# Another order of all units in a sorted-block attention and gated MLP kernel, with other PSUM banks and copying engines

## The chip, the core and the metric

The kernel runs on one core of one Trainium2 chip. A core has a matrix engine (TensorE, "PE"), a vector engine (VectorE, "DVE"), a scalar engine (ScalarE, "ACT"), GpSimd ("POOL") and a queue engine (SyncE, "SP"); each runs its own instruction stream in order, and the streams wait for each other by semaphores. TensorE writes its results to PSUM, eight banks, from which VectorE or ScalarE must copy them out before a bank can be used again. The metric is the device time of one execution in microseconds, less is better.

## The reference

Two layers, one after the other. First, attention within sorted blocks (batch 4, 8 heads, 768 tokens, head size 64, 8 blocks of 96 tokens): a small 8x8 matrix P per head is made from `sort_net`, and it mixes the blocks of K and V; each block of queries then attends to its mixed block.

```python
for _ in range(5):
    P = exp(P - max(P)); P = P / P.sum(-1); P = P / P.sum(-2)
k_sorted = einsum('bhij,bhjcd->bhicd', P, k_b); v_sorted = einsum(..., P, v_b)
attn = softmax(scale * q_b @ k_sorted^T)   # per block
x = (attn @ v_sorted)                      # 4 x 768 x 512
h = relu(x @ w_in); u, v = h[..., :512], h[..., 512:]
v_n = (v - mean(v)) / sqrt(var(v) + 1e-6)
v_s = w_spatial @ v_n + b_spatial          # over the tokens
out = (u * v_s) @ w_out
```

Inputs and outputs are float32; matmuls run on bfloat16.

## The kernel before, in words

The kernel is written as small *units*, each a Python function `u_XX`. The string `ORDER` at line 18 lists them, with arguments; `run` (line 805) calls them one by one, and nothing reorders the instructions afterwards, so on every engine an instruction stands where its unit stands in the string. A unit with matmuls names its PSUM place first (0 to 3 are pairs of banks, 10 to 17 single banks, of which 10 and 11 are pair 0, 12 and 13 pair 1, and so on), then the engine that copies the result out (A for ScalarE, D for VectorE), then the batch and the part. For example `UP:2:A:0:0:1` makes one block of U in pair 2, and ScalarE takes it out.

The units, in the order in which one batch needs them:

- `S0`, `SK`: load `sort_net`, then five rounds of normalising it on VectorE with an exp on ScalarE (line 248). `DM` (line 236) runs dummy matmuls on a tile `warm` meanwhile. `PR` (line 266) spreads P, `P0` (line 280, VectorE, batch 0) and `PD` (line 292, GpSimd, the other batches, from `prep_sb`, which `PC` copies) build the mixing matrices `pd`.
- `L`, `LH`: loads. All `L` loads are issued by GpSimd and cast to bfloat16 on the way (line 177 for q, k and v; 182 and 185 for the two halves of `w_in`, `wv` and `wu`; 191 for the two halves of `w_spatial`; 194 for `w_out`). `BI` (line 206) loads the bias `b_bc`.
- q, turned: batches 0 and 1 by TensorE (`QT`, line 325); batches 2 and 3 by a copy `QP` into `qp` (line 374, through the helper at line 122 or 124) and one DMA transpose `QX` on the SP queue (line 381).
- `KT` (line 394): K mixed and turned, 24 matmuls, into `kt_all`.
- V, mixed: batch 0 by `VT` and `VB` (lines 394 and 412); the others by `VM` (line 421) into `vm`, and `VC`, eight small DMAs on the SP queue (line 434), into `vb`.
- `SC` (line 453): scores of one head pair and half, then the exp on ScalarE (line 458) into one of five `ex_all` tiles. `AT` (line 499): attention times V, divided by its sum on VectorE (lines 506 and 507), into `x_sb`.
- x, turned: batch 0 by TensorE (`XT`, line 529), the others by DMA transposes `XD` on the SP queue (line 517).
- `VP`, `VH` (line 566): the V half of the first layer for one tile of tokens, then relu. `ST` (lines 586 and 587), `LN` (592, 593) and `LA` (598): the normalisation. `UP` (line 612): the U half. `WT`, `WW` (lines 535 and 542): the spatial weights, turned.
- `SP` (line 624): the spatial layer, then the bias on VectorE (line 630) into `z`. `GT` (line 641): times U, on VectorE or GpSimd. `OP` (line 650): the output layer, `OE` copies it out, `OS` (line 665) stores it, on the SP queue or, with a last `A`, from ScalarE's.
- The last batch's end is cut finer: `SH`, `GH`, `OH`, `OI`, `OJ` (lines 680, 693, 700, 707 to 714, 718).

The batches overlap: while batch b goes through the MLP, batch b + 1 is in attention, and the string interleaves them by hand-set numbers. The helpers `copy` (lines 120 to 124) and `relu` (126 to 130) hold most copies out of PSUM, so their rows carry those lines.

```python
    def run(order):
        for item in order.split():
            name, *args = item.split(":")
            units[name](*args)
```

Of the kernel before, what the change touches and what calls it, by code (L numbers as in the profile page):

```python
# [15 lines left out]

ORDER = """
S0 CO LH:A:0 TB L:q:0:4:8 SK:0 DM:10:3:384 DM:10:4:512 DM:10:13:512 BH ID IV:0 L:v:0:0:8 MC MA SK:1 DM:10:4:256 SK:2
QC:A:0 SK:3 SK:4 QC:A:1 QT:10:A:0:2 IV:2 QT:11:A:0:3 DM:12:4:512 QT:12:A:0:0 DM:13:6:512 PR:10 MB P0:0:2 P0:2:4  # L20
VT:2:A:0:0 VT:3:D:0:1 P0:4:6 QT:11:A:0:1 P0:6:8 VB:13:A:0:0 VB:12:D:0:1 L:k:0:0:8 PC:A VT:2:A:0:2 KT:3:D:0:1
KT:1:A:0:2 KT:0:A:0:3 VT:2:D:0:3 SC:3:0:1:1 KT:1:D:0:0 SC:0:0:2:0 VB:14:D:0:2 SC:3:0:3:0 L:k:1:0:8 AT:1:0:1:1
SC:0:0:0:0 L:v:1:0:8 PD:1:0:4 VB:15:D:0:3 SC:3:0:1:0 AT:1:0:2:0 SC:0:0:2:1 AT:2:0:3:0 SC:3:0:0:1 PD:1:4:8 AT:1:0:0:0
KT:0:A:1:0 XT:14:D:0:0:2 AT:3:0:0:1 SC:1:0:3:1 KT:0:A:1:3 AT:2:0:2:1 VM:1:A:1:0 AT:3:0:3:1 VM:0:A:1:1 VM:2:D:1:3
L:q:1:0:8 VM:1:A:1:2 XT:16:A:0:1:2 L:wv AT:0:0:1:0 XT:17:A:0:1:0 KT:2:D:1:1 KT:1:A:1:2 QT:16:D:1:1 QT:10:D:1:3
QT:11:A:1:2 QT:17:D:1:0 XT:14:D:0:0:0 SC:1:1:1:0 L:wsa SC:0:1:2:1 SC:3:1:2:0 VP:15:D:0:4 ST:0:4 VP:14:D:0:3 L:wu
SC:1:1:0:0 SC:0:1:1:1 VP:15:D:0:1 L:wsb ST:0:3 WT:16:A:1 WT:17:D:0 VP:14:A:0:0 ST:0:1 VH:15:A:0:2 ST:0:0 WT:16:A:2
VC:1:0:4 L:q:2:0:8 VH:17:A:0:5 VC:1:4:8 PD:2:0:4 ST:0:2 ST:0:5 AT:1:1:0:0 LN:0:0:6 AT:0:1:1:0 UP:2:A:0:0:0
UP:3:A:0:1:0 BI LA:0:3 LA:0:4 AT:1:1:2:0 SC:2:1:0:1 UP:0:A:0:1:1 LA:0:1 AT:3:1:2:1 L:v:2:0:8 WT:14:A:3 L:k:2:0:8
LA:0:5 LA:0:2 WW:1:D:4 LA:0:0 SC:0:1:3:1 SC:3:1:3:0 UP:2:A:0:0:1 PD:2:4:8 AT:0:1:3:1 QP:A:2:0 SP:1:0:3 QP:A:2:3  # L30
AT:3:1:3:0 QP:A:2:2 AT:2:1:0:1 QP:A:2:1 SP:0:0:0 AT:1:1:1:1 SP:3:0:2 VM:2:A:2:2 XD:1:0 VM:0:A:2:1 GT:D:0:0 SP:1:0:1
VM:3:D:2:0 GT:P:0:1 VM:2:A:2:3 VH:10:A:1:0 ST:1:0 KT:1:A:2:0 KT:2:D:2:1 KT:3:A:2:3 QX:2:0:4 KT:0:D:2:2 XD:1:1
UP:1:A:1:1:0 VH:16:D:1:1 SC:2:2:2:0 SC:0:2:0:0 VC:2:0:4:0:4 ST:1:1 GT:P:0:2 SC:1:2:3:0 VH:17:D:1:3 L:wo UP:2:A:1:1:1
AT:0:2:2:0 VH:16:A:1:4 AT:1:2:0:0 GT:P:0:3 VH:17:D:1:5 SC:2:2:1:0 L:q:3:0:8 SC:0:2:0:1 SC:1:2:1:1 VH:16:A:1:2 ST:1:3
UP:2:A:1:0:0 ST:1:5 AT:0:2:3:0 ST:1:4 ST:1:2 UP:1:A:1:0:1 LN:1:0:6 OP:3:0:2:2 LA:1:5 LA:1:1 SC:2:2:3:1 L:v:3:0:8
SC:0:2:2:1 PD:3:4:8 LA:1:0 OP:1:0:4:2 PD:3:0:4 LA:1:3 LA:1:2 OE:A:0:2 LA:1:4 L:k:3:0:8 QP:D:3:0 VC:2:4:8:0:4 OE:A:0:4
AT:2:2:3:1 SP:0:1:3 QP:A:3:3 AT:3:2:1:0 AT:1:2:2:1 QP:A:3:1 SP:2:1:1 AT:0:2:1:1 QP:A:3:2 VM:3:A:3:1 OP:1:0:0:2
OE:D:0:0 OS:0:0:0:1:A OS:0:0:1:2:A VM:2:A:3:3 AT:3:2:0:1 SP:0:1:2 VM:1:A:3:0 GT:P:1:1 XD:2:0 VM:3:D:3:2 SP:2:1:0
VH:16:D:2:2 QX:3:0:4 KT:0:A:3:0 KT:1:D:3:2 KT:2:D:3:3 KT:3:A:3:1 XD:2:1 VH:10:D:2:0 SC:1:3:0:1 ST:2:2 SC:3:3:0:0
SC:2:3:3:1 VC:3:4:8:0:4 OS:0:4:0:1 OS:0:4:1:2 VH:11:D:2:4 VH:10:A:2:5 AT:1:3:0:1 GT:P:1:3 VH:16:D:2:3 ST:2:3 ST:2:5  # L40
GT:P:1:2 SC:2:3:1:1 SC:0:3:2:1 SC:1:3:1:0 VH:17:A:2:1 GT:D:1:0 UP:2:A:2:1:0 AT:0:3:2:1 UP:1:A:2:1:1 ST:2:1 AT:3:3:1:1
ST:2:4 AT:2:3:3:1 UP:0:A:2:0:1 ST:2:0 UP:1:A:2:0:0 VC:3:0:4:0:4 AT:3:3:0:0 LN:2:0:6 LA:2:2 OP:0:1:0:2 OE:A:1:0 LA:2:4
AT:2:3:1:0 OP:1:1:4:2 LA:2:5 SC:3:3:2:0 LA:2:0 LA:2:3 LA:2:1 SC:0:3:3:0 OP:2:1:2:2 AT:3:3:3:0 SP:0:2:1 GT:D:2:1
OE:A:1:4 XD:3:1 AT:1:3:2:0 SP:3:2:0 SP:0:2:2 CK XD:3:0 GT:P:2:0 OE:A:1:2 SP:2:2:3 VH:1:D:3:5:3 GT:D:2:3 VH:10:D:3:4
UP:3:A:3:1:1 CF:11 VH:12:A:3:2 VH:13:A:3:1 OS:1:2:0:1 OS:1:2:1:2 LF VH:16:A:3:0 GT:D:2:2 OS:1:0:0:1:A OS:1:0:1:2:A
UP:2:A:3:1:0 ST:3:1 ST:3:3 UP:0:A:3:0:0 ST:3:4 ST:3:5 OP:1:2:0:2 ST:3:2 ST:3:0 OP:3:2:4:2 LN:3:0:6 LA:3:3 OE:D:2:0
LA:3:4 OP:2:2:2:2 LA:3:0 LA:3:1 OE:A:2:2 LA:3:5 UP:0:A:3:0:1 OE:A:2:4 LA:3:2 OS:0:2:0:1 OS:0:2:1:2 SH:12:3:2:0
SH:13:3:3:0 GH:P:3:3:0 SH:16:3:0:0 GH:D:3:2:0 SH:17:3:1:0 GH:P:3:0:0 SH:16:3:1:1 SH:12:3:2:1 OS:2:4 GH:P:3:1:0
SH:13:3:3:1 OS:2:0 GH:D:3:1:1 SH:17:3:0:1 OS:1:4 GH:D:3:3:1 OS:2:2 GH:P:3:0:1 GH:P:3:2:1 IF OH:16:3:2:0:512:0:4
OI:A:3:2:0:512 OH:12:3:3:0:512:0:4 OH:13:3:0:0:512:0:4 OI:D:3:0:0:512 OI:A:3:3:0:512 OH:17:3:1:0:512:0:4  # L50
OJ:3:2:0:512:S OJ:3:3:0:512:A OI:A:3:1:0:512 OJ:3:0:0:512:S OH:16:3:4:256:512:0:4 OI:D:3:4:256:512 OH:12:3:5:0:256:0:4
OI:D:3:5:0:256 OJ:3:1:0:512:S OJ:3:4:256:512:A OH:13:3:5:256:512:0:4 OJ:3:5:0:256:S OI:D:3:5:256:512
OH:17:3:4:0:128:0:4 OH:10:3:4:128:256:0:4 OI:B:3:4:0:256 OJ:3:5:256:512:S OJ:3:4:0:256:A
"""

# [791 lines left out]
```

## Time and profile before

| what | value |
|---|---|
| time, median of 3 runs (lowest, highest) | 149.85 us (149.81, 150.05) |
| the profiled execution's own time | 150.1 us |
| its span | 148.2 us |
| VectorE, ScalarE, GpSimd busy in the span | 114.6, 85.7, 39.1 us |
| granted TensorE clock | 1.0 of full |
| DMA moved | 25.94 MB, 175 GB/s on average |

How to read it: the page gives busy times of the engines, the span cut into 40 slices, and the chain of work that ended last, followed back from the last instruction. Further views list the instructions of one engine in order of time, the groups by line, the waits by what ended them, and each DMA's time from issue to landing. Times of rows are microseconds from the start of the span. A row that ends in square brackets tells how long the engine had been idle ahead of it and whom it waited for. TensorE's weight loads are counted apart (PEld).

### The profile page before, as it was taken

To read this page: it belongs to the slowest core of one execution; us is meant where nothing else is said; L and a number is where in the kernel's file an instruction comes from. 1 tells how busy PE (TensorE), PEld (TensorE's weight loads), DVE (VectorE), ACT (ScalarE), POOL (GpSimd) and SP (SyncE) were. 2 spreads that over 40 slices of the span, in tenths; PEclk is the share of its full clock that TensorE was granted. 3 is DMA by queue.
4 is the path that set the end of the run, shared out by engine and by line. 5 is a ranking of instruction groups with operands and counts; after the bars stand their busy time and mean duration, and the time that the engine had idled before them with its cause. 6 is when DMAs were issued, how large, how long until landed. Compare 5 with 4: busy or idle time off the path is not lost.

```text
span 148.2 us, 4112 instructions
## 1 busy us (share of the span) xinstructions
PE 142.2 (96%) x1689; PEld 101.1 (68%) x1691; DVE 114.6 (77%) x262; ACT 85.7 (58%) x126; POOL 39.1 (26%) x44
## 2 busy tenths in 40 slices
PE   6997999999999999999999999999999999999991
PEld 2355877866776667777877678768866876864760
DVE  3876899979987887867869779899558989846741
ACT  5347998997689546659693328756640046160040
POOL 6700599500000005992001640000002100004630
PEclk9999999999999999999999999999999999999999
DMA  3999999999999999799999999503602607007766
GB/s 93 263 203 204 204 208 201 209 218 242 234 248 216 209 215 237 110 172 221 205 201 178 206 243 286 118 0 73 38 0 56 194 3 283 2 2 264 296 224 221
DMA packets 37014, 25.94 MB, mean 175 GB/s; under 512 B 16704, under 2 KB 34112, under 8 KB 36992
## 3 DMA queue, kind: packets, MB, share of 16 engines
q0 software_dynamic: 14432, 12.19, 51.6%
...
q8 instruction: 14, 0.23, 0.6%
...
## 4 chain that ended last, share of the span: by engine, by line
PE 90%; DVE 6%; ACT 1%; issue 1%; DVEq 0%
PE ps L624 16%; PE ps L566 15%; PE ps L612 14%; PE ps L650 11%; PE ps L236 6%; PE ps L680 5%; PE ps L499 4%; PE ps L394 4%; PE ps L453 4%; PE ps L700 4%; PE ps L421 3%; DVE x_sb L507 2%; PE ps L325 2%; DVE vb L124 1%; PE ps L535 1%; PE ps L529 1%
## 5 line engine op out<-in xcount | busy, mean ns | idle before, releaser
L641 POOL TENSOR_TENSOR gt<-z,u_sb 128x768 bf16<-128x768 f32 x7 | 11.4, 1644 | 68.8 <-DVE z L630 55.5
L458 ACT ACTIVATE ex_all<-ps 96x768 bf16<-96x768 f32 x32 | 23.7, 807 | 5.0 <-PE ps L453 4.0
L624 PE MATMUL ps<-wspT,v_sb 128*128 128x384 bf16 x144 | 25.0, 326 | 0.0
L566 PE MATMUL ps<-w_in_sb,xT 128*128 128x256 bf16 (+1 forms) x175 | 23.7, 282 | 0.1
L612 PE MATMUL ps<-xT,w_in_sb 128*128 128x384 bf16 x128 | 23.0, 326 | 0.0
L128 ACT ACTIVATE u_sb<-ps 128x768 bf16<-128x768 f32 x16 | 13.0, 811 | 17.3 <-PE ps L612 17.2
L507 DVE TENSOR_TENSOR x_sb<-ps,rec_all 96x512 bf16<-96x512 f32 x32 | 22.0, 686 | 1.1
L624 PEld LDWEIGHTS <-v_sb 128*128 128x128 bf16 x144 | 13.5, 98 | 8.4
L566 PEld LDWEIGHTS <-xT 128*128 128x128 bf16 x176 | 16.3, 98 | 4.0
L650 PE MATMUL ps<-w_out_sb,gt 128*128 128x256 bf16 x144 | 16.9, 273 | 0.0
L612 PEld LDWEIGHTS <-w_in_sb 128*128 128x128 bf16 x128 | 12.0, 98 | 7.0
L586 DVE BATCH_NORM_STATS2 stats<-v_sb 128x6 f32<-128x512 bf16 x24 | 16.2, 675 | 0.6 <-ACT v_sb L128 0.5
L122 ACT COPY o_sb<-ps 128x1024 f32<-128x1024 f32 (+2 forms) x11 | 8.9, 830 | 12.6 <-PE ps L700 9.3
L630 DVE TENSOR_TENSOR z<-ps,b_bc 128x768 f32<-128x768 f32 x12 | 11.5, 954 | 5.9 <-PE ps L624 5.1
L650 PEld LDWEIGHTS <-gt 128*128 128x128 bf16 x144 | 13.8, 98 | 2.0
L499 PEld LDWEIGHTS <-ex_all 96*128 96x128 bf16 x256 | 11.1, 97 | 2.6
L499 PE MATMUL ps<-vb,ex_all 96*128 96x65 bf16 x256 | 12.3, 193 | 0.1
L122 ACT CAST vm<-ps 128x768 bf16<-128x768 f32 x9 | 6.8, 807 | 9.7 <-PE ps L421 6.6
L236 PE MATMUL ps<-warm 128*128 128x512 bf16 (+2 forms) x33 | 9.6, 451 | 1.3 <-DVE warm L210 1.3
L693 POOL TENSOR_TENSOR gt<-z,u_sb 128x512 bf16<-128x512 f32 (+1 forms) x5 | 5.2, 1047 | 21.5 <-DVE z L686 21.5
L506 DVE RECIPROCAL rec_all<-ps 96x8 f32<-96x8 f32 x32 | 6.3, 196 | 5.5 <-PE ps L499 5.3
L130 DVE TENSOR_SCALAR v_sb<-ps 128x512 bf16<-128x512 f32 (+1 forms) x12 | 8.7, 727 | 1.6 <-PE ps L566 1.5
...
## 6 DMA issues: line engine op xcount, KB each, us to landing
...
vb<-vm SPq DMA_DIRECT2D x24, 99.0 KB, 4.7
...
```

What stands on the lines that cost most here:

```text
L122: nc.scalar.copy(out=out, in_=in_)
L128: nc.scalar.activation(out=out, in_=in_, func=AF.Relu)
L236: nc.tensor.matmul(t[:, 0, 0:int(w)], lhsT=warm[:, 0:128], rhs=warm[:, 0:int(w)], start=True, stop=True)
L458: nc.scalar.activation(out=e_tile(b, hp, ih).rearrange("p h (x g) -> p h x g", g=G), in_=t[0:BLK, :, 0:HW].rearrange("p h (g x) -> p h x g ...
L499: nc.tensor.matmul(t[:, hh, ii * VW:ii * VW + D + 1], lhsT=e[:, c:c + 128], rhs=vb[b % 2][:, ih * NI + ii, 2 * hp + hh, 0:D + 1], start=Tr ...
L507: nc.vector.tensor_mul(out=x_sb[:, hp].rearrange("p i (h d) -> p h i d", h=2), in0=tv[:, :, :, 0:D], in1=_raw_ap(rec, 0, [rec.ap[0], [NI, ...
L566: nc.tensor.matmul(t[:, x, c:c + DH // parts], lhsT=st["xT", b][:, n // 3, kc, (n % 3) * 128:(n % 3 + 1) * 128], rhs=w_in_sb[:, kc, DH + c ...
L586: nc.vector.bn_stats(out=stats, in_=st["v_sb", b, n])
L612: nc.tensor.matmul(t[:, x, 0:HW], lhsT=w_in_sb[:, kc, mc * 128:(mc + 1) * 128], rhs=st["xT", b][:, ih, kc, :], start=(kc == 0), stop=(kc = ...
L624: nc.tensor.matmul(t[:, x, 0:HW], lhsT=st["v_sb", b, n][:, mc * 128:(mc + 1) * 128], rhs=wspT[:, 3 * x:3 * x + 3, n, :], start=(n == 0), s ...
L630: nc.vector.tensor_add(out=z.rearrange("p (x c) -> p x c", x=2), in0=t[:, :, 0:HW], in1=b_bc.rearrange("p (x c) -> p x c", x=2),)
L650: nc.tensor.matmul(t[:, x, c:c + w], lhsT=st["gt", b, mc][:, (n0 + x) * 128:(n0 + x + 1) * 128], rhs=w_out_sb[:, mc, c:c + w], start=(mc = ...
```

## The change

Only the string `ORDER` differs. The same work is listed in another sequence, with other banks and other copying engines: against before, ScalarE has two `KT` more, two of the `UP` less, and VectorE one `VB`, one `QT`, one `XT` and the `PC` copy more, and four single-tile and the one double relu of the V half less. The dummies `DM` are regrouped. `WW`, which turned two parts of the spatial weights into one pair, is two `WT`. Stores of the first batches that stood on the SP queue stand in ScalarE's stream, later. `L:wv` and `L:wu` stand next to each other. The core of the diff, its first and fourth line:

```diff
-S0 CO LH:A:0 TB L:q:0:4:8 SK:0 DM:10:3:384 DM:10:4:512 DM:10:13:512 BH ID IV:0 L:v:0:0:8 MC MA SK:1 DM:10:4:256 SK:2
+S0 CO IV:0 DM:10:3:384 DM:10:3:512 IV:2 LH:A:0 TB SK:0 L:q:0:4:8 BH ID MA DM:10:12:512 SK:1 DM:10:1:128 SK:2 QC:A:0
...
-L:q:1:0:8 VM:1:A:1:2 XT:16:A:0:1:2 L:wv AT:0:0:1:0 XT:17:A:0:1:0 KT:2:D:1:1 KT:1:A:1:2 QT:16:D:1:1 QT:10:D:1:3
+XT:15:D:0:1:0 VM:3:A:1:0 VM:1:A:1:2 XT:14:D:0:0:2 L:wv L:wu VM:0:D:1:1 XT:15:D:0:0:0 KT:3:A:1:1 QT:14:D:1:3
```

Three places, as the instructions stand on the engines. First VectorE behind the last round on P (`p_t`), up to the copies of the first K and V tiles (`-` before, `+` now, neither: in both):

```order
 L261 STREAM_TRANSPOSE p_t<-p_75 32x64
+L124 COPY qT<-ps 128x768
 L224 CAST mask_89<-m_88 128x16
-L280 TENSOR_TENSOR pd<-mask_89,ps 128x256 x2
+L280 TENSOR_TENSOR pd<-mask_89,ps 128x256 x4
+L124 CAST prep_sb<-ps 128x256
 L124 CAST vt_all<-ps 128x768
-L280 TENSOR_TENSOR pd<-mask_89,ps 128x256 x2
 L124 COPY vb_97<-ps 96x8x2x64
-L124 CAST kt_all<-ps 128x768
+L124 CAST kt_all<-ps 128x768 x2
+L124 COPY vb_97<-ps 96x8x2x64
```

A qT copy now stands ahead of the mask; the four `P0` stand together with the `prep_sb` copy behind them and ahead of the first `vt_all`.

Second, GpSimd's loads in the middle of the start, from the mixing matrices of batch 1 to the load of q for batch 2:

```order
-L292 TENSOR_TENSOR pd<-mask_89,prep_sb 128x512 x2
+L292 TENSOR_TENSOR pd<-mask_89,prep_sb 128x512 x3
 L177 DMA q_in<-in_q_dram 128x8x384
 L182 DMA w_in_sb<-in_moe_w_in_dram 128x4x512
-L191 DMA ws_in<-in_moe_w_spatial_dram 128x3x768
 L185 DMA w_in_sb<-in_moe_w_in_dram 128x4x512
-L191 DMA ws_in<-in_moe_w_spatial_dram 128x3x768
+L191 DMA ws_in<-in_moe_w_spatial_dram 128x3x768 x2
+L206 DMA b_bc<-in_moe_b_spatial_dram 128x768
 L177 DMA q_in<-in_q_dram 128x8x384
```

The two halves of `w_in` are still two instructions, now one behind the other; both halves of `w_spatial` and the bias follow; a third half of `pd` is made ahead of them.

Third, ScalarE around the copies of q for batch 3 (`qp`) and its V (`vm`), before:

```order
L592 ACTIVATE rstd<-mv,eps 128x6
L593 ACTIVATE rstd<-rstd 128x6
L458 ACTIVATE ex_all<-ps 96x768 x2
L122 COPY o_sb<-ps 128x1024 x2
L122 COPY qp<-q_in 128x2x6x64 x3
L122 CAST vm<-ps 128x2x6x64
L665 DMA out_dram<-o_sb 128x512 x2
L122 CAST vm<-ps 128x2x6x64 x2
```

and now:

```order
L122 COPY o_sb<-ps 128x1024
L458 ACTIVATE ex_all<-ps 96x768
L122 COPY qp<-q_in 128x2x6x64
L128 ACTIVATE u_sb<-ps 128x2x384
L122 CAST vm<-ps 128x2x6x64
L122 COPY qp<-q_in 128x2x6x64
L122 CAST vm<-ps 128x2x6x64
L122 COPY qp<-q_in 128x2x6x64
L122 CAST vm<-ps 128x2x6x64
```

The three `qp` copies of ScalarE (VectorE makes the fourth in both) stood together ahead of V; now they alternate with the `vm` copies, and the last stands behind the second of these. The two stores are gone from here.

More of the change, by code (lines that the diff above doesn't have):

```diff
@@ L18 @@
 ORDER = """
-S0 CO LH:A:0 TB L:q:0:4:8 SK:0 DM:10:3:384 DM:10:4:512 DM:10:13:512 BH ID IV:0 L:v:0:0:8 MC MA SK:1 DM:10:4:256 SK:2
[L20 to L23, printed above, removed]
@@ L24 @@
-KT:0:A:1:0 XT:14:D:0:0:2 AT:3:0:0:1 SC:1:0:3:1 KT:0:A:1:3 AT:2:0:2:1 VM:1:A:1:0 AT:3:0:3:1 VM:0:A:1:1 VM:2:D:1:3
-L:q:1:0:8 VM:1:A:1:2 XT:16:A:0:1:2 L:wv AT:0:0:1:0 XT:17:A:0:1:0 KT:2:D:1:1 KT:1:A:1:2 QT:16:D:1:1 QT:10:D:1:3
-QT:11:A:1:2 QT:17:D:1:0 XT:14:D:0:0:0 SC:1:1:1:0 L:wsa SC:0:1:2:1 SC:3:1:2:0 VP:15:D:0:4 ST:0:4 VP:14:D:0:3 L:wu
-SC:1:1:0:0 SC:0:1:1:1 VP:15:D:0:1 L:wsb ST:0:3 WT:16:A:1 WT:17:D:0 VP:14:A:0:0 ST:0:1 VH:15:A:0:2 ST:0:0 WT:16:A:2
-VC:1:0:4 L:q:2:0:8 VH:17:A:0:5 VC:1:4:8 PD:2:0:4 ST:0:2 ST:0:5 AT:1:1:0:0 LN:0:0:6 AT:0:1:1:0 UP:2:A:0:0:0
@@ L29 @@
[L29 to L53, printed above, removed]
+S0 CO IV:0 DM:10:3:384 DM:10:3:512 IV:2 LH:A:0 TB SK:0 L:q:0:4:8 BH ID MA DM:10:12:512 SK:1 DM:10:1:128 SK:2 QC:A:0
@@ new lines @@
+SK:3 SK:4 MC QT:10:A:0:2 QT:11:A:0:3 DM:12:13:512 L:v:0:0:8 QT:12:D:0:0 PR:10 MB DM:11:2:256 P0:0:2 P0:2:4 P0:4:6
+QC:A:1 VT:2:A:0:0 P0:6:8 QT:11:A:0:1 PC:D VT:3:D:0:1 VB:13:D:0:0 L:k:0:0:8 VT:2:A:0:3 KT:0:D:0:1 KT:3:A:0:3 KT:1:D:0:2
+KT:2:A:0:0 SC:0:0:1:1 VB:16:D:0:1 SC:1:0:3:0 VT:2:D:0:2 SC:0:0:3:1 VB:17:D:0:3 L:k:1:0:8 SC:1:0:0:0 L:v:1:0:8 PD:1:0:4
+AT:2:0:1:1 SC:0:0:0:1 PD:1:4:8 VB:16:D:0:2 SC:1:0:2:0 PD:2:0:4 AT:2:0:3:0 KT:0:A:1:3 AT:3:0:0:0 SC:1:0:2:1 AT:2:0:3:1
+KT:0:A:1:0 AT:3:0:0:1 SC:1:0:1:0 AT:2:0:2:1 L:q:1:0:8 KT:0:A:1:2 AT:3:0:2:0 VM:1:A:1:3 XT:14:A:0:1:2 AT:0:0:1:0
@@ new lines @@
+XT:15:D:0:1:0 VM:3:A:1:0 VM:1:A:1:2 XT:14:D:0:0:2 L:wv L:wu VM:0:D:1:1 XT:15:D:0:0:0 KT:3:A:1:1 QT:14:D:1:3
+QT:12:A:1:1 L:wsa QT:13:D:1:2 L:wsb QT:10:D:1:0 SC:3:1:3:0 SC:2:1:1:0 BI L:q:2:0:8 SC:1:1:2:0 SC:0:1:3:1 VP:16:D:0:1
+VP:17:A:0:5 ST:0:1 VP:14:D:0:2 VP:15:A:0:0 VH:16:A:0:4 VH:17:A:0:3 UP:1:A:0:0:1 ST:0:5 WT:16:A:2 WT:17:A:1 ST:0:0
+ST:0:2 ST:0:4 L:v:2:0:8 VC:1:0:4 ST:0:3 AT:0:1:1:0 AT:2:1:3:0 UP:1:D:0:1:0 LN:0:0:6 LA:0:4 SC:0:1:0:1 LA:0:0 LA:0:3
+SC:3:1:2:1 UP:2:A:0:0:0 WT:10:D:4 WT:11:A:3 AT:1:1:2:0 VC:1:4:8 WT:16:D:5 LA:0:1 WT:17:A:0 SC:2:1:0:0 SC:0:1:1:1
@@ new lines @@
+LA:0:2 UP:1:A:0:1:1 LA:0:5 QP:A:2:0 AT:3:1:2:1 QP:A:2:2 L:k:2:0:8 SP:2:0:0 QP:A:2:1 AT:0:1:0:0 AT:3:1:3:1 SP:1:0:1
+PD:2:4:8 AT:2:1:0:1 XD:1:0 AT:0:1:1:1 SP:3:0:3 GT:P:0:3 VM:1:D:2:1 QP:A:2:3 VM:2:A:2:3 SP:0:0:2 L:wo VM:3:A:2:0
+VM:2:A:2:2 VH:12:A:1:0 VH:13:D:1:1 KT:3:A:2:2 QX:2:0:4 KT:0:A:2:3 L:v:3:0:8 KT:2:D:2:1 KT:1:A:2:0 ST:1:1 VH:16:D:1:2
+GT:D:0:1 PD:3:4:8 SC:0:2:1:0 XD:1:1 PD:3:0:4 SC:2:2:2:0 VC:2:0:4:0:4 SC:1:2:3:0 VH:17:D:1:4 VH:0:A:1:5:3 ST:1:2 ST:1:5
+UP:2:A:1:1:0 SC:3:2:3:1 ST:1:4 SC:1:2:0:0 VC:2:4:8:0:4 GT:D:0:2 GT:P:0:0 UP:0:A:1:0:1 ST:1:0 ST:1:3 UP:2:A:1:1:1
@@ new lines @@
+LN:1:0:6 AT:3:2:2:0 OP:1:0:0:2 AT:0:2:1:0 LA:1:0 AT:2:2:3:0 LA:1:5 OP:3:0:2:2 OE:A:0:0 SC:1:2:1:1 SC:0:2:2:1 LA:1:1
+OP:2:0:4:2 LA:1:3 L:q:3:0:8 OE:A:0:4 OE:D:0:2 AT:1:2:0:0 L:k:3:0:8 SC:0:2:0:1 LA:1:4 QP:A:3:1 UP:3:A:1:0:0 VM:2:A:3:2
+LA:1:2 QP:D:3:2 AT:1:2:1:1 SP:0:1:2 QP:A:3:0 VM:3:A:3:1 AT:2:2:3:1 SP:1:1:1 XD:2:0 AT:0:2:0:1 AT:3:2:2:1 QP:A:3:3
+SP:2:1:0 QX:3:0:4 GT:P:1:1 VM:1:A:3:0 VM:0:D:3:3 VH:16:A:2:2 XD:2:1 KT:2:A:3:3 KT:1:A:3:2 KT:0:D:3:0 KT:3:D:3:1
+SP:2:1:3 VH:10:A:2:1 ST:2:2 VC:3:4:8:0:4 SC:1:3:3:1 SC:3:3:0:1 SC:2:3:2:1 VC:3:0:4:0:4 VH:11:A:2:4 VH:10:A:2:5
@@ new lines @@
+GT:D:1:2 AT:1:3:3:1 GT:P:1:3 ST:2:1 UP:3:A:2:1:0 GT:D:1:0 VH:14:D:2:3 SC:1:3:1:0 SC:0:3:1:1 ST:2:3 SC:3:3:0:0
+VH:15:A:2:0 OP:1:1:0:2 ST:2:4 ST:2:5 AT:0:3:2:1 OE:A:1:0 ST:2:0 AT:3:3:1:1 UP:2:A:2:0:0 LN:2:0:6 LA:2:0 LA:2:4
+OP:1:1:2:2 OE:A:1:2 LA:2:2 AT:0:3:0:1 LA:2:5 UP:2:D:2:1:1 LA:2:1 LA:2:3 SC:3:3:3:0 SC:1:3:2:0 UP:0:A:2:0:1 AT:2:3:3:0
+OS:0:2:0:1:A OS:0:2:1:2:A AT:3:3:0:0 OS:0:4:0:1:A OS:0:4:1:2:A SP:1:2:3 AT:0:3:1:0 SP:2:2:2 AT:3:3:2:0 OS:1:2:0:1:A
+OS:1:2:1:2:A GT:D:2:2 XD:3:1 SP:1:2:1 XD:3:0 UP:0:A:3:0:1 GT:D:2:3 CK SP:2:2:0 OP:3:1:4:2 VH:10:A:3:3 CF:11
@@ new lines @@
+VH:1:A:3:0:1 VH:11:D:3:5 ST:3:3 GT:P:2:0 ST:3:1 OE:A:1:4 ST:3:0 VH:2:A:3:4:2 GT:P:2:1 OP:1:2:4:2 UP:0:A:3:1:1 ST:3:2
+UP:3:A:3:1:0 LF ST:3:4 ST:3:5 LN:3:0:6 LA:3:5 OE:A:2:4 LA:3:0 LA:3:4 OS:1:0:0:1:A OS:1:0:1:2:A OP:2:2:2:2 LA:3:2
+LA:3:1 OE:A:2:2 LA:3:3 OP:0:2:0:2 OE:A:2:0 OS:0:0:0:1 OS:0:0:1:2 UP:3:A:3:0:0 SH:14:3:2:0 SH:15:3:3:0 GH:P:3:3:0
+SH:14:3:0:0 GH:D:3:2:0 SH:15:3:1:0 GH:P:3:0:0 SH:14:3:1:1 SH:16:3:2:1 OS:2:4 GH:P:3:1:0 SH:15:3:3:1 OS:2:0 GH:D:3:1:1
+SH:14:3:0:1 OS:1:4 GH:D:3:3:1 OS:2:2 GH:P:3:0:1 GH:P:3:2:1 IF OH:17:3:2:0:512:0:4 OI:A:3:2:0:512 OH:16:3:3:0:512:0:4
@@ L54 @@
+OH:15:3:0:0:512:0:4 OI:D:3:0:0:512 OI:A:3:3:0:512 OH:14:3:1:0:512:0:4 OJ:3:2:0:512:S OJ:3:3:0:512:A OI:A:3:1:0:512
+OJ:3:0:0:512:S OH:17:3:4:256:512:0:4 OI:D:3:4:256:512 OH:16:3:5:0:256:0:4 OI:D:3:5:0:256 OJ:3:1:0:512:S
+OJ:3:4:256:512:A OH:15:3:5:256:512:0:4 OJ:3:5:0:256:S OI:D:3:5:256:512 OH:14:3:4:0:128:0:4 OH:10:3:4:128:256:0:4
+OI:B:3:4:0:256 OJ:3:5:256:512:S OJ:3:4:0:256:A
 """
```

## The prediction

> **What bounds the kernel now.** I read the page first, then the chain of work that ended last, because it says on which engine a saving would count.
>
> ```profile
> span 148.2 us, 4112 instructions
> PE 142.2 (96%) x1689; PEld 101.1 (68%) x1691; DVE 114.6 (77%) x262; ACT 85.7 (58%) x126; POOL 39.1 (26%) x44
> PE   6997999999999999999999999999999999999991
> ```
>
> TensorE is busy for 96% of the span, and its slices show the only thin places: the first four of forty and the last. The chain, in order of time (start, length, what), says where that begins:
>
> ```profile
> 1.28 7.15 PE ps L236 x24
> 8.43 0.79 PE ps L325 x24
> ...
> 10.65 1.40 PE ps L236 x6
> ...
> 25.33 0.04 issue
> 25.38 0.48 PE ps L421 x2
> ...
> 30.84 0.70 PE ps L453 x24
> 31.54 0.32 PE ps L566
> ...
> 95.51 1.30 PE ps L612 x8
> ...
> 139.69 5.22 PE ps L700 x36
> 144.91 0.02 issue
> ```
>
> From 25.38 to 144.91 us every piece is TensorE: 119.5 us without a wait. The change removes no work there: both orders hold the same matmuls, apart from dummies on L236. So from 25 us on a new order **can only lose**, by making TensorE wait. It can win only ahead of that, where the chain runs through VectorE and ScalarE, which copy out of PSUM what TensorE made.
>
> **Part 1, the start.** VectorE from its first use of the mixing matrix to the first layer of the MLP (start, length; in brackets the idle time ahead):
>
> ```profile
> 12.44 0.75 DVE L280 TENSOR_TENSOR pd<-mask,ps 128x256 bf16<-128x256 bf16 x2 [0.74 <-PE ps L266]
> ...
> 13.82 0.96 DVE L124 CAST vt_all<-ps 128x768 bf16<-128x768 f32 x1 [0.62 <-PE ps L394]
> ...
> 15.56 0.69 DVE L124 COPY vb<-ps 96x1024 bf16<-96x1024 bf16 x1
> 15.90 0.37 ACT L122 CAST prep_sb<-ps 128x256 bf16<-128x256 f32 x1
> ...
> 17.64 0.96 DVE L124 CAST vt_all<-ps 128x768 bf16<-128x768 f32 x1 [0.40 <-PE ps L394]
> ...
> 28.82 0.94 DVE L124 CAST kt_all<-ps 128x768 bf16<-128x768 f32 x1
> 29.69 1.47 DVE L124 COPY qT<-ps 128x768 bf16<-128x768 bf16 x3
> ...
> 31.08 0.54 DVE L124 COPY xT<-ps 128x768 bf16<-128x768 bf16 x1
> ```
>
> It is packed from 12.44 to 31.62 but for two holes, 0.62 and 0.40. In the same stretch the new order gives VectorE all of what it had, plus the cast of prep_sb, one vb copy and one more xT copy, minus one kt copy: 0.37 + 0.69 + 0.54 − 0.94 = +0.66. (prep_sb has a ScalarE row only. Its price on VectorE is not shown: 0.37 or a little less would follow from half of the L280 pair, which writes as much, and 0.96 at most from the three times wider casts; I take 0.37.) Against that, all four L280 now stand together with the cast behind them, ahead of the first vt copy. That is work for the hole of 0.62 that waits for a matmul. So VectorE ends at 31.62 + 0.66 − 0.62 = 31.66; if the 0.40 goes too, 31.26; if neither is filled, 32.28.
>
> When does the stretch start? Before, 24 dummies end at 8.43. The new order has 1,920 fewer columns of them ahead of the first transposes; by the six that took 1.40 (3,072 columns) that is 0.88, so 7.55. Then 24 transposes (0.79), 13 dummies of 512 (3.03), 12 transposes (half of 0.79), then a qT copy that VectorE now makes itself (0.49, a third of the 1.47) and the mask (0.1, a choice: its row is not shown): 7.55 + 0.79 + 3.03 + 0.40 + 0.49 + 0.1 = 12.36. So L280 starts about as before, at 12.4. The first transposes also wait for the q load, which GpSimd now issues behind the filling of two tiles; nothing waited for it before, so I allow 0.2 for it, a choice.
>
> TensorE cannot start the first layer before the fourth score block of batch 1, and that waits for VectorE's last qT copy. A block is a third of the 0.70 at 30.84. So the layer starts at 31.66 + 0.23 = 31.89, against 31.54 now; but the new order has then done four score blocks and not three, so 31.77 would be equal. **Start: +0.1** (−0.3 to +0.7 by the holes, up to +0.9 with the late q).
>
> **Part 2, the loads.** The two halves of the weights stay two transfers; only the order of issue changes, wv, wu, then both parts of the spatial weights.
>
> ```profile
> 20.86 0.81 POOL L185 DMA_DIRECT2D w_in_sb<-in_moe_w_in_dram  x1
> ...
> DMA to landing us min/median/max: 10.8/13.6/16.4
> ```
>
> The third load of the four landed at 20.86 + 16.4 = 37.3. In the new order the third is the first spatial half, of about the same size. Its first use comes behind six V tiles of 0.87 (row below) and one U block of 1.30: 31.9 + 5.2 + 1.3 = 38.4. The margin of 1.1 covers it, and wu has moved earlier, ahead of its earlier use. **Zero**; each us by which it lands after 38.4 would be paid in full. GpSimd also makes a third pd block ahead of the q load, which delays its issue by about 1.1; that load stands behind others that had not landed, so it is hidden.
>
> **Part 3, the fourth batch.** Its V is mixed on TensorE, copied to vm, spread by eight small DMAs on the SP queue (vb), and used by the first attention block. The SP queue runs one thing after another: the turned q (qT), the second xT of batch 2, then vb.
>
> ```profile
> 80.53 3.57 SPq L381 DMA_TRANSPOSE qT<-qp  x1
> 84.20 2.48 SPq L517 DMA_TRANSPOSE xT<-x_sb  x1
> 86.78 2.58 SPq L434 DMA_DIRECT2D vb<-vm  x4
> ```
>
> Issue to landing of each (the first row is the same qT of batch 2):
>
> ```profile
> qT<-qp SPq DMA_TRANSPOSE x1, 5.1
> ...
> qT<-qp SPq DMA_TRANSPOSE x1, 8.4
> ...
> xT<-x_sb SPq DMA_TRANSPOSE x1, 5.9
> ...
> vb<-vm SPq DMA_DIRECT2D x4, 99.0 KB, 3.4
> ```
>
> And the rows that stand between, on TensorE and then ScalarE:
>
> ```profile
> 82.34 1.95 PE ps L624 x12
> 84.29 0.65 PE ps L421 x4
> ...
> 86.94 0.87 PE ps L566 x8
> 87.81 1.46 PE ps L394 x48
> ...
> 90.25 0.69 PE ps L453 x24
> 90.94 1.85 PE ps L566 x16
> 92.80 0.24 PE ps L499 x8
> ```
>
> ```profile
> 76.04 2.31 ACT L122 COPY qp<-q_in 128x768 bf16<-128x768 bf16 x3
> ...
> 83.98 1.50 ACT L122 CAST vm<-ps 128x768 bf16<-128x768 f32 x2 [3.12 <-DVE x_sb L507]
> ```
>
> In the present order all qp copies are done at 78.35 and the SP queue has slack. In the new one the last qp copy stands behind the second vm copy of batch 3. Call T the end of the matmuls for that copy. ScalarE needs 0.75 and 0.77, so qT issues at T + 1.6; the xT at T + 1.6 + 3.57 = T + 5.2; vb at T + 5.2 + 2.48 = T + 7.7. Its fourth part, three quarters of 2.58 later, lands at T + 7.7 + 1.9 + 3.4 = T + 13.0. TensorE meanwhile does three attention blocks (0.72), three spatial blocks (5.85), two vm (0.65), one V tile, four kt (1.46), another V tile (1.74 for both), three scores (0.69) and two more tiles (1.85): it asks for vb at T + 13.0. That is just in time. qT lands by T + 10.0 and is asked for at T + 10.4; xT lands by T + 11.1, asked for at T + 11.1. All three fit, with nothing left on the last two at the longer latencies. **I take +0.1, between 0 and +0.4**, the 0.4 for half an xT issue or a qp copy that is late (the 0.77) by half.
>
> The 8.4 above fell together with two output stores that ScalarE issued; the 5.1 had none beside it:
>
> ```profile
> 83.07 0.87 ACTq L665 DMA_DIRECT2D out_dram<-o_sb  x2
> ```
>
> The new order sends those stores out near the end of the program. The Trainium skill, page "DMA: Bandwidth & Descriptors", section "Issuing engines are not separate DMA queues", says that transfers from any issuing engine run on the same 16 DMA engines and interleave, so that another queue saves only issue time. By that rule taking the stores away in time, and not the queue that issues them, is what counts: the qT would take 5.1 again, and part 3 would cost nothing (150.0 in all). By the slower rows it is up to +0.4. I stay with +0.1.
>
> **Part 4, small things.** In batch 1 a score block follows two weight transposes in the same PSUM pair, whose copy on ScalarE ends about when it starts: 0.05, between 0 and 0.2. Six stores stand in a row in ScalarE's stream behind batch 2's last U block, 0.43 each by the row above: 2.6 us, hidden, since three spatial blocks (5.85) come on TensorE ahead of the next copy that ScalarE has to make. The tail has the same shapes in other banks: zero.
>
> **Sum.** 0.1 + 0 + 0.1 + 0.05 = +0.25. The profiled execution took 150.1 us for its span of 148.2, so 1.9 lies around it; the new span is 148.45, 150.35 in that execution. It ran 0.25 above the median of 149.85, so on the median's scale I predict **150.1 us**.
>
> **The rivals.**
> 1. *The start gains.* Both holes of VectorE close, and copies of a kind run closer: three qT took 0.49 each, the lone xT of the same shape 0.54, and some six copies more now have a neighbour (0.05 each, 0.3). For it: the order has VectorE's copies side by side, and no vb copy is left on ScalarE ahead of the kt copies. Against: VectorE has 0.66 more to do. Price −0.3 to −0.6: 149.4. It decides if the last qT copy ends ahead of 31.3.
> 2. *The start loses* (the slower side). L280 waits for VectorE's own qT copy, which waits for 13 dummies behind a late q load; nothing fills the holes. Price +0.7 to +0.9: 150.65. It decides if L280 starts after 12.65, or the last qT copy ends after 32.2.
> 3. *Batch 3's V is late.* vb lands after T + 13.0 and TensorE stands at the first attention block. Price +0.4 beside the +0.15 of the other parts: 150.4. It decides if the qT issues later than T + 1.6.
> 4. *Nothing of the weights' order shows*: the two halves still land one after another, so it doesn't do what it says. That is in my forecast already, at zero.
>
> **How the numbers follow.** What a measurement can tell from no change is about 0.2%, 0.3 us. My forecast (149.9 to 150.4) gets 0.44; rival 1, 0.23; rival 2, 0.20; rival 3, 0.13. Of the forecast some 0.26 lies within the 0.3 and 0.16 above, 0.02 below. Together: faster 0.25, same 0.29, slower 0.46. The range takes rival 1's low end (149.85 − 0.6 = 149.25) and the three high ends together (0.9 + 0.4 + 0.2 = 1.5): 149.2 to 151.4.
>
> **What would show it.** The chain should again be TensorE alone from about 25.5 us to the end. Step 1: the first L566 starts near 31.9, VectorE's last qT copy ends near 31.7, L280 starts at 12.4 to 12.6. Step 2: no wait of L535 for a DMA. Step 3: between the kt block of the fourth batch and its first attention block TensorE idles for no more than 0.1. I would be wrong in kind if the waits name TensorE idle after 32 us anywhere else: a bank still held by a copy, or batch statistics that VectorE delivers late.

## The result, and the profile after

The new order takes 153.5 us in the median of five runs (151.68 to 161.37), against 150.05 of the order before in the same session: 1.0155 times as long, 95% interval 1.0117 to 1.0193. That is outside the range on record. The five of the new order lie 9.7 us apart, the five of before 0.3 us (of the executions of before beside the later experiments one took 153.66, so one long execution alone proves little). The profiled one is the longest (161.37, span 159.6), and the ratio leaves the two longest out. So the next rows show the fault at its largest; an execution of the usual length follows with the experiments.

The page of the profiled execution after, with the slices of TensorE's busy share and of its granted clock:

```profile
span 159.6 us, 4115 instructions
PE 145.1 (91%) x1691; PEld 102.1 (64%) x1691; DVE 113.1 (71%) x261; ACT 87.4 (55%) x127; POOL 37.4 (23%) x43
...
PE   6997999999999996039999999999999999999991
...
PEclk9999999999999999556999999999999999999999
```

Before, the middle of the first row of digits was all nines. Now there is a hole between 60 and 72 us, and the clock stands at half for three slices. The first row of TensorE's waits after (line, whom it waited for, sum, times, longest) names it; in before no wait for a DMA was on that list:

```profile
PE ps L566 <- DMA xT<-x_sb: 8.2, 1, 8.2
```

In the chain after, in order of time, there are now pieces that are not TensorE:

```profile
7.82 0.79 PE ps L325 x24
8.61 2.91 PE ps L236 x13
...
12.80 0.43 DVE pd L280
...
32.34 7.67 DMA vb<-vm
40.05 0.55 PE ps L499 x13
...
57.49 12.98 DMA xT<-x_sb
70.52 4.88 PE ps L566 x24
```

The second turned x of batch 1 was issued at 57.49 and took 13 us; TensorE stood for 8.15 of them. Then 24 matmuls took 4.88 us, where 0.87 per eight is the undisturbed price (2.6). So of the 11.4 us that the span grew, 8.2 are that wait, and 2.9 are TensorE's busy time (145.1 against 142.2); these 24 matmuls at the lower clock make 2.3 of the 2.9. The Trainium skill, page "TensorE: Matmul & The Clock Gate", section "What's actually happening", says that an idle window of about 3.4 us halves the clock until about as long a stretch of work has passed. The trace agrees in kind: the granted clock was 1.00 from 60 to 62 us, 0.65 in the mean to 70.5, 0.50 to 73 and 0.69 to 76. From these means, taking the clock as either full or half, I estimate about 10.3 us at half clock, from some 2 us after TensorE stopped to some 4 us after it started again, which is near the page's 3.4 and not equal to it.

Why 13 us? In before the same transpose landed in 3.5. Here are the two queues around it. SP before, then GpSimd before:

```profile
56.24 1.42 SPq L517 DMA_TRANSPOSE xT<-x_sb  x1
```

```profile
57.09 3.25 POOL L641 TENSOR_TENSOR gt<-z,u_sb 128x768 bf16<-128x768 f32 x2 [27.38 <-DVE z L630]
60.28 0.82 POOL L194 DMA_DIRECT2D w_out_sb<-in_moe_w_out_dram  x1
...
63.65 0.88 POOL L177 DMA_DIRECT2D v_in<-in_v_dram  x1
```

and the same two after:

```profile
57.49 1.75 SPq L517 DMA_TRANSPOSE xT<-x_sb  x1
```

```profile
55.65 1.64 POOL L641 TENSOR_TENSOR gt<-z,u_sb 128x768 bf16<-128x768 f32 x1 [24.36 <-DVE z L630]
57.23 0.81 POOL L194 DMA_DIRECT2D w_out_sb<-in_moe_w_out_dram  x1
58.04 0.89 POOL L177 DMA_DIRECT2D v_in<-in_v_dram  x1
```

Before, the load of `w_out` stood on GpSimd behind two `gt` products and was issued 4.0 us after the transpose, when that had landed. In the new order one `gt` stands ahead of it, so that it is issued 0.26 us ahead of the transpose, and the load of v for batch 3 follows at once. What the DMA engines moved shows the rest (queue, packets, megabytes). In before, from 56 to 59 us, the transposes' queue alone; after, from 60 to 69 us, both queues:

```profile
q1 hardware_dynamic: 2794, 0.71, 102.2%
```

```profile
q0 software_dynamic: 1406, 1.19, 91.2%
q1 hardware_dynamic: 1405, 0.36, 38.0%
```

Alone, the transposes move 0.71 MB in 3 us, 237 KB per us with the pause between two of them. Beside the loads (q0) the two queues send as many packets each, 1406 and 1405 in 9 us; a load's packet is 0.85 KB, a transpose's 0.25, so the transposes get 40 KB per us. The loads' first packets moved between 59.25 and 59.5 us, the transpose's only from 60.0 on, so the whole of it ran beside them. The Trainium skill, page "DMA: Bandwidth & Descriptors", section "Queues, rings and completion order", says that a DMA engine goes round its queues and changes at packets; the equal counts in this execution agree.

### The profile page after: what moved, and what is told of

It is laid out like the page before. It is cut to its first block, busy times and chain, and to the rows that moved or that the text cites. A ratio compares the mean times of both kernels' runs of the same rounds, so it can differ in the third digit from the quotient of the medians.

```text
span 159.6 us, 4115 instructions
## 1 busy us (share of the span) xinstructions
PE 145.1 (91%) x1691; PEld 102.1 (64%) x1691; DVE 113.1 (71%) x261; ACT 87.4 (55%) x127; POOL 37.4 (23%) x43
## 4 chain that ended last, share of the span: by engine, by line
PE 70%; DMA 13%; DVE 10%; issue 2%; SPq 1%; POOL 1%; ACT 1%; DVEq 0%; POOLq 0%
PE ps L612 13%; PE ps L624 11%; PE ps L650 10%; PE ps L566 10%; DMA xT<-x_sb 8%; PE ps L236 6%; PE ps L680 5%; DVE x_sb L507 5%; DMA vb<-vm 5%; PE ps L700 3%; PE ps L499 3%; PE ps L453 3%; PE ps L394 3%; DVE z L630 1%; SPq L434 1%
## 5 line engine op out<-in xcount | busy, mean ns | idle before, releaser
L566 PE MATMUL ps<-w_in_sb,xT 128*128 128x256 bf16 (+1 forms) x176 | 24.9, 299 | 8.2 <-DMA xT<-x_sb 8.2
L641 POOL TENSOR_TENSOR gt<-z,u_sb 128x768 bf16<-128x768 f32 x6 | 9.8, 1639 | 85.3 <-DVE z L630 55.2
L566 PEld LDWEIGHTS <-xT 128*128 128x128 bf16 x176 | 17.9, 104 | 13.7 <-DMA xT<-x_sb 8.3
L128 ACT ACTIVATE v_sb<-ps 128x512 bf16<-128x512 f32 (+1 forms) x14 | 9.6, 694 | 21.4 <-PE ps L566 21.4
L128 ACT ACTIVATE u_sb<-ps 128x768 bf16<-128x768 f32 x14 | 11.4, 812 | 12.7 <-DVE z L630 7.4
L122 ACT COPY o_sb<-ps 128x1024 f32<-128x1024 f32 (+2 forms) x12 | 10.0, 843 | 12.6 <-PE ps L700 10.2
L612 PEld LDWEIGHTS <-w_in_sb 128*128 128x128 bf16 x128 | 11.8, 98 | 7.1
L630 DVE TENSOR_TENSOR z<-ps,b_bc 128x768 f32<-128x768 f32 x12 | 11.4, 951 | 5.3 <-PE ps L624 4.3
L130 DVE TENSOR_SCALAR v_sb<-ps 128x512 bf16<-128x512 f32 x7 | 4.8, 688 | 13.7 <-PE ps L566 13.6
L499 PE MATMUL ps<-vb,ex_all 96*128 96x65 bf16 x256 | 12.0, 193 | 0.3 <-DVE x_sb L507 0.2
L499 PEld LDWEIGHTS <-ex_all 96*128 96x128 bf16 x256 | 10.6, 97 | 2.4 <-issue 0.2
L236 PE MATMUL ps<-warm 128*128 128x512 bf16 (+3 forms) x34 | 9.9, 457 | 1.3 <-DVE warm L210 1.3
L598 DVE TENSOR_SCALAR v_sb<-v_sb,mv,rstd 128x512 bf16<-128x512 bf16 x24 | 8.5, 404 | 1.5 <-ACT rstd L593 1.5
```

The lines of the kernel that those rows point to most:

```text
L122: nc.scalar.copy(out=out, in_=in_)
L128: nc.scalar.activation(out=out, in_=in_, func=AF.Relu)
L236: nc.tensor.matmul(t[:, 0, 0:int(w)], lhsT=warm[:, 0:128], rhs=warm[:, 0:int(w)], start=True, stop=True)
L499: nc.tensor.matmul(t[:, hh, ii * VW:ii * VW + D + 1], lhsT=e[:, c:c + 128], rhs=vb[b % 2][:, ih * NI + ii, 2 * hp + hh, 0:D + 1], start=Tr ...
L566: nc.tensor.matmul(t[:, x, c:c + DH // parts], lhsT=st["xT", b][:, n // 3, kc, (n % 3) * 128:(n % 3 + 1) * 128], rhs=w_in_sb[:, kc, DH + c ...
L612: nc.tensor.matmul(t[:, x, 0:HW], lhsT=w_in_sb[:, kc, mc * 128:(mc + 1) * 128], rhs=st["xT", b][:, ih, kc, :], start=(kc == 0), stop=(kc = ...
```

## The experiments

**The theory**: GpSimd's loads now bring their data while the xT transpose runs. Whether they do would then be decided by a few tenths of a microsecond between two queues, and that would make the scatter. **The rivals**: the start has lost; the weights' loads cost it; batch 3's V is late.

**e0**: the changed kernel again, with no edit.

> The changed kernel once more, nothing altered. Main theory (GpSimd's loads wo and v3 start just ahead of the second xT transpose of batch 1, and the transpose then shares the DMA engines with them packet by packet): the time scatters between about 151.5 and 161, and in every execution the transpose issued near 57.5 us takes 8 to 14 us to land instead of the 3.5 us of before, with an idle time of TensorE ahead of an L566 that grows with it. Rival (the start alone has lost): about 151 to 152 in every execution, and the idle time before that L566 belongs to the one long execution seen.

151.86 us (151.03 to 152.64), 1.0109 times before (1.0065 to 1.0154). The profiled execution took 152.23. Its waits of TensorE:

```profile
PE ps L566 <- DMA xT<-x_sb: 1.4, 1, 1.4
...
PE ps L499 <- DMA vb<-vm: 0.3, 1, 0.3
```

The load was issued 0.24 us *after* the transpose here, at 56.97 against 56.73, and the chain has the transpose at

```profile
56.73 6.68 DMA xT<-x_sb
```

It is the same wait in a smaller size, but not quite the same picture. The DMA queues from 58 to 59.5 us, and then from 60 to 63 us:

```profile
q1 hardware_dynamic: 1314, 0.34, 96.2%
```

```profile
q0 software_dynamic: 409, 0.42, 109.5%
q1 hardware_dynamic: 31, 0.00, 1.4%
```

Here the transpose's data started at about 58 us, ahead of the load's (59.5), and all but some 30 of its packets were through by 60. It landed at 63.41 all the same: those last packets trickled beside the load, far fewer than one for each of the load's. So the equal counts of the first profile are no general rule, and why the last packets took over 3 us stays open. Half a microsecond between the two issues goes with a wait of 1.4 instead of 8.2; that it alone makes the difference is not shown. The transpose stayed under the 8 us that the theory gave as its least, and the time reached lower than its 151.5: the race is lost by less here than in the first profile.

**e1**: the two loads behind the `pd` blocks of batch 3; all other engines as in the changed kernel.

```diff
-SP:0:0:2 L:wo VM:3:A:2:0
+SP:0:0:2 VM:3:A:2:0
...
-KT:0:A:2:3 L:v:3:0:8 KT:2:D:2:1
+KT:0:A:2:3 KT:2:D:2:1
...
-PD:3:0:4 SC:2:2:2:0
+PD:3:0:4 L:wo L:v:3:0:8 SC:2:2:2:0
```

> The changed order, but on GpSimd the loads wo and v3 stand behind the two pd blocks of batch 3 (issued near 59.4 and 60.2 us instead of 57.2 and 58.0); every other engine's order is that of the changed kernel. Main theory: the second xT of batch 1 lands within about 4 to 6 us, no L566 waits for it for more than 0.5 us, the scatter goes, and what is left against before is the start's 0.4 to 0.7 us: 150.4 to 150.9. Rival (the weights' order, the start or batch 3's V make the loss): still 152 and above, with the same scatter.

150.99 us (150.65 to 152.01), 1.0074 (1.0047 to 1.0100): 0.9 us less than e0 on the same chip, and six of the seven executions lie within 0.7 us. The two intervals overlap, so that e1 is faster rests as much on the wait that is gone from its trace as on the times. One issue from each of its two queues, and the longest waits of TensorE beside its dummies' start:

```profile
56.69 1.42 SPq L517 DMA_TRANSPOSE xT<-x_sb  x1
```

```profile
59.27 0.82 POOL L194 DMA_DIRECT2D w_out_sb<-in_moe_w_out_dram  x1
```

```profile
PE ps L325 <- DMA q_in<-in_q_dram: 0.5, 1, 0.5
PE ps L499 <- DMA vb<-vm: 0.5, 1, 0.5
PE ps L394 <- DVE pd L280: 0.3, 1, 0.3
```

The load is issued 2.6 us behind the transpose, which lands in 3.5 again, and no L566 waits. The theory's number was 150.4 to 150.9, just missed; and the scatter is smaller, not gone (one execution took 152.01).

**e7**: as e1, but only v3 moved; wo stays where the change has it.

```diff
-KT:0:A:2:3 L:v:3:0:8 KT:2:D:2:1
+KT:0:A:2:3 KT:2:D:2:1
...
-PD:3:0:4 SC:2:2:2:0
+PD:3:0:4 L:v:3:0:8 SC:2:2:2:0
```

> The changed order, v3 moved behind the two pd blocks, wo left where the change has it (issued near 57.0 us). Main theory (any load that brings its data while the xT transpose runs slows it): wo alone is enough, the xT takes 5 to 13 us to land, time and scatter as the changed kernel's, 151.3 to 153. Rival (the sum of wo and v3 makes it, or only v3's smaller packets): as the run with both moved, 150.7 to 151.1.

152.96 us (151.53 to 158.15), 1.0155 (1.0109 to 1.0201), with the wait in the profile again:

```profile
PE ps L566 <- DMA xT<-x_sb: 1.6, 1, 1.6
```

The load was issued at 57.06, 0.10 us behind the transpose, which took 6.8 us to land. The 512 KB of `w_out` alone are enough; size and scatter are like the change's own. (It ran on another chip than e0 and e1, so only its ratio to before is compared.)

**e4**: the old order with only these two loads early.

```diff
+L:wo L:v:3:0:8
 GT:P:0:1
...
-L:wo
...
-L:v:3:0:8
```

> The order of before, with nothing of the change but this: on GpSimd the loads wo and v3 stand ahead of the first of its gt blocks (near 57 us instead of 60.3 and 63.7). Main theory: the xT transpose issued at 56.2 us, which took 3.5 us, now takes 8 us or more, TensorE idles ahead of an L566 of batch 1, and the kernel takes 152 to 158 us with a scatter of its own. Rivals: no change from before within 0.3 us.

169.03 us (168.33 to 169.41), 1.1263 (1.1224 to 1.1301). In direction as the theory says, in size far more, and for a reason that I had not seen: in that place GpSimd waits only 0.7 and 2.3 us ahead of the two loads, so they went out at 30.9 and 34.1, not near 57. So this is not the change's own case, but one with the loads 29 us early. They lay behind others in the software queue (wo landed 25.9 us later), so that loads ran without a break to about 61 us, through every transpose of the stretch:

```profile
PE ps L566 <- DMA xT<-x_sb: 13.5, 2, 7.7
```

From 55 to 59 us the queues moved

```profile
q0 software_dynamic: 742, 0.58, 92.2%
q1 hardware_dynamic: 706, 0.18, 34.3%
```

which is 45 KB per us for the transposes, one packet for one again. 13.5 us of waits and 5.2 of TensorE's busy time (147.4 against 142.2, with slices of the granted clock at 5, 7 and 5 tenths) make the 18.7 by which the span grew.

**e9**: the old order with the weights' loads alone changed.

```diff
-L:wv
+L:wv L:wu
...
-VP:14:D:0:3 L:wu
+VP:14:D:0:3
```

> The order of before with nothing of the change but the loads of the input weights: wv and wu side by side, then both spatial parts. Expected by every theory but one: no difference from before within 0.3 us. The rival that the weights' order itself costs time (a spatial part that lands after its transposes ask for it): slower by 0.3 us or more, with a wait of L535 for a DMA.

152.22 us (151.99 to 153.78), 1.0158 (1.0120 to 1.0197). I had expected nothing. TensorE's rows:

```profile
34.15 1.04 PE L566 MATMUL ps<-w_in_sb,xT 128*128 128x512 bf16 x4
36.74 0.84 PE L535 MATMUL ps<-ident,ws_in 128*128 128x128 bf16 x12 [1.55 <-DMA ws_in<-in_moe_w_spatial_dram]
```

In the old order of units the spatial part is asked for at 35.2 and lands at 36.7. That is 1.5 of the 2.3 us between the medians; in the profile another 0.4 lies in the start, where the 24 dummies ahead of the first transposes took 7.56 us instead of 7.15, which the edit doesn't touch. So the rival is right there; what is left to ask is whether it is in the new order too.

**e5**: e1 with the weights' loads in the old sequence.

```diff
-L:wv L:wu
+L:wv
...
-L:wsa
+L:wsa L:wu
```

> The run with wo and v3 behind the pd blocks, and the weights' loads in the order of before (wv, first spatial part, wu, second). In the old order of units, wv and wu side by side cost 1.5 us, because L535 asked for the spatial part at 35.2 us and it landed at 36.7. In the new order L535 asks at 38.5. Theory (the new order of units hides the weights' order): within 0.3 us of that run, 150.7 to 151.2, no wait of L535 in either. Rival (wv and wu side by side cost or gain something here too): a difference of 0.4 us or more.

151.75 us (150.90 to 153.43), 1.0093 (1.0057 to 1.0130). Its interval overlaps e1's, the profiled executions of both have a span of 149.2, and L535 waits in neither. No gain from undoing the weights' order: the new order of units asks for the spatial part at 38.5 and hides it. The medians differ by 0.8, in two sessions on one chip; that is more than the theory's 0.3, no wait in the two profiles accounts for it, and it is left unexplained.

**e2**: e1 with another start.

```diff
-DM:12:13:512 L:v:0:0:8 QT:12:D:0:0
+DM:12:11:512 L:v:0:0:8 QT:12:A:0:0
```

> As the run with the loads behind the pd blocks, and in the start qT's third copy goes to ScalarE instead of VectorE and 11 dummies of 512 stand ahead of it instead of 13. Theory of the start (VectorE's own qT copy, behind 13 dummies, holds L280 until 12.8 us): L280 starts at 12.0 to 12.4 and the first L566 0.4 to 0.7 us earlier than in that run, so 149.8 to 150.3. Rival (the start is bound by the q load or by VectorE's copies behind L280, not by its first one): no more than 0.1 us of difference between the two runs.

151.01 us (150.66 to 151.40), 1.0066 (1.0042 to 1.0089): no change against e1. My theory of the start fell. L280 starts at 12.23, against 12.30 in e1: in both the matmuls of L266 ahead of it start at 11.8, behind ScalarE's qT copies. The 12.80 of the first profile, from which I had made the theory, began with the 19 dummies ahead of the first transposes. The first profile, then e1:

```profile
1.28 6.54 PE L236 MATMUL ps<-warm 128*128 128x384 bf16 x19 [1.28 <-DVE warm L210]
```

```profile
1.28 5.44 PE L236 MATMUL ps<-warm 128*128 128x384 bf16 x19 [1.28 <-DVE warm L210]
```

The q landed at 7.3 and 7.2 us, about alike; the dummies of the first profile ended behind it, at 7.82, and all that follows up to L280 was later. Why the same dummies take 1.1 us longer in one execution stays open: the granted clock stands at 1.00 in both. The first layer was even later in e2, at 32.24 against 32.07.

**e6** and **e10** tried the wait of L499 for batch 1's vb (0.5 us in e1). e6 puts a U block ahead of the first two attention blocks, e10 the last V block ahead of an xT:

```diff
-AT:0:1:1:0 AT:2:1:3:0 UP:1:D:0:1:0
+UP:1:D:0:1:0 AT:0:1:1:0 AT:2:1:3:0
```

```diff
-XT:14:D:0:0:2 L:wv L:wu VM:0:D:1:1
+VM:0:D:1:1 XT:14:D:0:0:2 L:wv L:wu
```

> The run with wo and v3 behind the pd blocks, and in batch 1 one U block (8 matmuls on L612, 1.46 us) ahead of its first two attention blocks instead of behind them. Theory of what is left in that run (batch 1's vm copies start 1.6 us later than before, so its vb lands just after TensorE asks for it, a wait of 0 to 0.5 us at L499 near 40 us): no wait of L499 for vb, 0.2 to 0.4 us less than that run's 150.99, so 150.6 to 150.8. Rival (the whole remainder lies in the start): no difference from that run.

> The run with wo and v3 behind the pd blocks, and in batch 1 the last V block and VectorE's copy of it to vm one place ahead of the xT block that stood before it. Theory (what is left in that run is 0.25 us of the start and 0.3 to 0.5 us in which L499 waits for batch 1's vb, whose issue waits for this last vm copy): the first vb issues 0.4 us earlier, the wait at L499 near 40 us goes, 150.4 to 150.7. Rival (the wait comes from the loads beside the vb transfers, not from their issue): the wait stays, 150.9 to 151.1.

e6: 152.83 us, 1.0200 (1.0149 to 1.0250). e10: 151.22 us, 1.0070 (1.0040 to 1.0101). Both take the wait away, and both bring another. Waits of TensorE in e6:

```profile
PE ps L453 <- DVE x_sb L507: 1.5, 1, 1.5
```

and in e10:

```profile
PE ps L325 <- DVE xT L124: 0.4, 1, 0.4
```

In e6 VectorE takes out the U block first, so the attention's bank comes free late; in e10 the q transposes wait for the bank of the xT that was moved back. So vb is late by 0.3 to 0.5 us in the new order, but its price in the whole was not measured by these two: each paid it in another place.

**e8**: the old order with fewer dummies.

```diff
-DM:13:6:512
+DM:13:4:512
```

> The order of before with 4 instead of 6 dummies of 512 ahead of the mixing matrix's matmuls. In before, L266 starts when the dummies end (11.98 us), and p_t has been ready since 11.64. Theory (the start is a chain through p_t, L266 and L280): L280 starts 0.3 us earlier and the kernel takes 149.75 to 149.9, 0.1 to 0.3 us less than before. Rival (VectorE's holes take it up, or the first layer waits for something else): no change.

149.87 against 149.92 us, 0.9999 (0.9977 to 1.0020). L280 starts 0.30 earlier (12.14) and TensorE ends 0.26 earlier (144.64 for 144.90) in the profile, but the runs can't tell the two kernels apart.

## Why the prediction was wrong

**The step that failed** is part 2. It asked of the loads only when the weights land, and whether GpSimd's third `pd` block delays a q load. That GpSimd also reaches its later loads sooner (wo by 3.05 us, v for batch 3 by 5.6), and that their data then runs beside a transpose for which TensorE waits, is in neither the sum nor a rival; the sum has it at zero. It cost 0.9 us in the usual execution (e0 against e1), and 8.2 us of waiting in the longest. With the loads moved back, the wait went (e1); `w_out` alone is enough for it (e7); with the loads put early into the old order, in another place and much earlier, it appears there (e4). What happens on the DMA engines in detail is shown for the longest execution and e4, and is open for the end of the transpose in e0.

Without this step e1's 150.99 lies inside the range on record, but above the forecast's 149.9 to 150.4: about +0.9 against before, where the sum had +0.25. So the rest of the prediction was too low as well, and the next points say where.

**What bounds the kernel**: right. From 25 us on nothing could be gained, and the loss came from a wait of TensorE, of the kind that the last part of the prediction named only in general ("anywhere else").

**Part 1, the start**: right in its mechanism, a little small. The hole of 0.62 did close. VectorE's rows in e1:

```profile
12.30 1.41 DVE L280 TENSOR_TENSOR pd<-mask,ps 128x256 bf16<-128x256 bf16 x4
13.63 0.42 DVE L124 CAST prep_sb<-ps 128x256 bf16<-128x256 f32 x1
14.01 0.96 DVE L124 CAST vt_all<-ps 128x768 bf16<-128x768 f32 x1
...
30.04 1.48 DVE L124 COPY qT<-ps 128x768 bf16<-128x768 bf16 x3
```

L280 starts at 12.30 (12.36 predicted), the prep_sb cast took 0.42 (0.37 taken), the last qT copy ends at 31.52 (31.66). That the start came out so near is in part luck: the forecast priced the first dummies by six later ones, and they took 5.4 to 6.5 us from one profile to another (5.44 in e1, 5.71 in e0, 6.54 in the first one). But the first layer starts at 32.07, not 31.89:

```profile
30.77 1.15 PE L453 MATMUL ps<-qT,kt_all 64*128 64x96 bf16 x32
32.07 5.36 PE L566 MATMUL ps<-w_in_sb,xT 128*128 128x512 bf16 x31 [0.15 <-ACT ex_all L458]
```

The four score blocks run in one piece, and the layer waits 0.15 for an exp to free a bank. Against the 31.77 that would be equal, +0.3, not +0.1. Rival 2's condition (L280 after 12.65) came true only in the first profile, and there by the slower dummies, not by a late q.

**Left out of part 1**: batch 1's vb. VectorE's vm copy comes at 28.71 and not at 26.98, the eight DMAs go out 1.6 us later, and TensorE waits up to 0.5 us for them at L499. SP before and in e1:

```profile
28.19 5.21 SPq L434 DMA_DIRECT2D vb<-vm  x8
```

```profile
29.76 6.04 SPq L434 DMA_DIRECT2D vb<-vm  x8
```

With the start's 0.3 that accounts for 0.8 of the 0.97 us by which TensorE ends later in e1's profile than in before's (145.87 for 144.90). This sum is read from one trace of each, and the start alone varies from execution to execution by as much as its term; only the places of the two terms, not their prices, were tried.

**Part 2's own numbers**: the weights' order cost nothing in the new order, as forecast. The first spatial part landed at 36.4 in e1 (37.3 predicted) and was asked for at 38.6 (38.4), so the margin was 2.1 and not 1.1 us. It hangs on the new order of units: in the old one the same order of loads made TensorE wait 1.5 us (e9).

**Part 3, batch 3**: right, to 0.3 us. ScalarE and SP in e0:

```profile
82.03 0.80 ACT L122 CAST vm<-ps 128x768 bf16<-128x768 f32 x1 [0.20 <-PE ps L421]
82.72 0.83 ACT L122 COPY qp<-q_in 128x768 bf16<-128x768 bf16 x1
```

```profile
83.58 3.03 SPq L381 DMA_TRANSPOSE qT<-qp  x1
86.95 2.50 SPq L517 DMA_TRANSPOSE xT<-x_sb  x1
89.55 5.14 SPq L434 DMA_DIRECT2D vb<-vm  x8
```

With T at 82.03, qT issues at T + 1.55 (1.6), xT at T + 4.9 (5.2), vb at T + 7.5 (7.7), and the first attention block starts at 94.84, T + 12.8 (13.0), without a wait. The qT took 6.1 us to land in e0 and 6.0 in e1, with no store issued beside it: nearer to the 5.1 than to the 8.4 us that the prediction weighed. Rival 3 did not come. The +0.1 that I gave for it was zero.

**Part 4** and **rival 1**: none of the waits in e0 or e1 is at the weight transposes, the stores or the tail, as forecast; the start gained nothing. **Rival 4** holds in the new order.
